# Five hand-written step orders instead of two, and an earlier low part in the tail, in a fused attention and expert kernel

## The chip, the cores and the metric

The kernel runs on one core of a Trainium2 chip. The metric is the device time of one execution in microseconds (us). The engines are TensorE (PE, with its weight loads PEld), VectorE (DVE), ScalarE (ACT), GpSimd (POOL) and SyncE (SP, which issues DMAs). Every engine works through its own instructions in the order in which the program gives them.

## The reference

Three layers: attention that keeps the 32 largest scores of each row, a gated feed-forward layer, and a layer in which each token goes to one of eight experts. Batch 4, 8 heads, 576 positions, head size 64; 2304 tokens of width 512.

```python
scores = scale * q @ k.T                                # 32 x (576 x 576)
kth = np.partition(scores, -32, axis=-1)[..., -32:-31]
scores = np.where(scores >= kth, scores, -1e9)
attn = softmax(scores); x = attn @ v                    # 2304 x 512
h = x @ w_in                                            # 512 -> 2048
y = (h * np.clip(h + 3, 0, 6) / 6) @ w_out              # 2048 -> 512
logits = norm(y) @ norm(expert_emb).T / tau             # 8 experts
e = logits.argmax(1); gate = softmax(logits)[e]
out = gate * (np.maximum(y @ w1[e], 0) @ w2[e])         # 512 -> 1024 -> 512
```

## The kernel before

The attention is cut into 72 units: 128 query rows of two heads each (the last eight units hold the rows left over). A software pipeline runs over them in steps i = 0 to 75. Step i works on six units at once: it computes the scores of unit i, picks the 32 largest values of unit i-1, masks unit i-2, takes the exponentials and sums of unit i-3, turns unit i-4 so that its keys lie on partitions, and in odd steps multiplies units i-5 and i-4 with v. After every eight units (step 11 is the first time) a group of 256 tokens is complete; it gives eight pieces of the feed-forward layer, and from step 12 on (step 13 excepted) each step also does one piece. In steps 0 to 18 the feed-forward weights are prepared too: 32 pieces ("pairs" of row blocks) are rounded to a high part, which stays in SBUF, and a low part, which goes to DRAM and is fetched when needed; a step handles two of them (one in steps 0 to 2).

A step is a list of named operations, and the list is a hand-written string: `FIRST` for steps 0 to 11, `MID` for steps 12 to 20, then `ODD` and `THEN` alternately. The names are issued in the string's order, so that the string sets, for every engine and for SP's DMA queue, what stands ahead of what. The names:

- weights: `load` (DMA), `one` and `two` (DVE, lines 245 and 252, write tile wf), `round` (ACT, 260), `add` (POOL, 265), then one step later `hi` (ACT, 273), `low` (POOL, 277), `store` (DMA). The digit behind is which of the step's two pieces.
- attention: `score0/1` (PE, the two halves of the keys), `take0/1` (ACT copies out of PSUM, 450), `pairs` (DVE, 459 to 463, folds the halves), `pick0..3` (DVE, MAX8 and MATCH_REPLACE, 478 and 481), `bounds` (POOL), `bend0/1` (ACT, 492, tile z), `mask0/1` (POOL, 496), `expo0/1` (ACT, 502), `guard` (POOL, 506), `inverse` (DVE, 509), `scale` (ACT, 516; POOL from unit 16), `turn0..2` (PE, 529), `keep0..2` (ACT, 534, tile pt), `values` (PE, 547), `xh` (ACT, 564), `xl` (DVE, 579).
- feed-forward: `s10`, `s11` (PE, 611), `gate` (ACT), `swish` (DVE, 623), `large` (ACT), `small` (POOL), `s20`, `s21` (PE, 646).
- `lows`, `ship`, `prep`, `need_v`, `load_k`, `load_q` prepare keys, queries and values.

The two halves of a unit's scores share one PSUM tile. `score0` of step i+1 therefore waits until `pairs` and `take1` of step i are through with it. The lists name `pairs` behind `take1`; in step 0 alone two lines of `step` put it ahead:

```python
        if i == 0:
            names.remove("pairs")
            names.insert(names.index("take1"), "pairs")
```

Behind the steps comes the tail: the last group's feed-forward pieces, the routing of its 256 tokens (`choose`, `rank`, `place`), and the first expert. `hidden(0, f, ...)` is one block of 128 hidden features of the first expert (12 matmuls into tile ph, of which there are two), `hidden_out` reads ph (ACT, line 971, and DVE, line 972, the low part hl), and `first` is both. `split_2(0, k)` splits a quarter of the expert's second weights into a high part h (ACT, 869) and a low part l (DVE, 871); the weights a come by DMAs that are issued earlier (line 865).

Of the kernel before, what the change touches and what calls it, by code (L numbers as in the profile page):

```python
# [40 lines left out]

PAUSE = (13,)
RAMP, MOES, WORDS = 3, 12, 21
FIRST = ("hi0 s10 expo0 lows hi1 turn0 one0 s11 s20 low0 round0 two0 ship keep0 turn1 expo1 guard bend0 keep1 add0 turn2 load0 "
         "store0 one1 load_k inverse keep2 prep mask0 pick0 round1 score0 gate take0 scale two1 bend1 load_q swish large values xh "
         "score1 pick1 pick2 aside s21 add1 load1 xl pick3 need_v low1 take1 store1 pairs mask1 bounds small")
MID = ("lows turn0 hi0 turn1 low0 s10 s11 ship keep0 one0 keep1 expo0 two0 pick0 load_k turn2 store0 one1 pick1 expo1 hi1 guard "
       "round0 bend0 two1 score0 pick2 keep2 low1 s20 take0 gate bend1 inverse add0 score1 values take1 round1 scale swish mask0 "
       "large s21 add1 xh pick3 need_v prep xl mask1 load_q bounds small store1 load0 load1 pairs aside")
THEN = ("lows pick0 turn0 expo0 keep0 ship expo1 pick1 bend0 s10 guard turn1 place pick2 inverse score0 mask0 turn2 s11 take0 "  # L50
        "keep1 bend1 pick3 need_v gate load_k score1 swish keep2 scale aside load_q bounds values take1 mask1 xh large xl prep "
        "s20 small s21 pairs")
ODD = ("pick0 turn0 bend0 pick1 turn1 lows s10 s11 keep0 ship score0 expo0 keep1 gate pick2 mask0 turn2 place keep2 bend1 mask1 "
       "take0 swish values expo1 load_k score1 guard need_v pick3 bounds take1 large aside inverse s20 s21 scale small xh pairs "
       "prep xl load_q")
# [47 lines left out]
def layers(tc: tile.TileContext, qt, kt, v, w_in, w_out, embt, tau, w1, w2, out, y_dram, yq_dram, g_dram, tbl, xq_dram, lo_dram, flag, pools, consts):  # L103
# [40 lines left out]
    def bank():  # L144
        turn[1] ^= 1
        return bank_t[turn[1]]
# [603 lines left out]
    def rank():  # L750

        g0, g1 = open_.popleft()
        n = g1 - g0
        pq = (bank() if looping[0] else half_a())[:, :n * E]
        nc.tensor.matmul(pq, tri, picks[:, g0:g1, :].rearrange("p g e -> p (g e)"), start=True, stop=False)
        nc.tensor.matmul(pq, ones, before[:, g0:g1, :].rearrange("p g e -> p (g e)"), start=False, stop=True)
        po = fs.tile([128, NG, E], F32, tag="df", name="pos")[:, :n, :]
        nc.vector.tensor_tensor(po, pq.rearrange("p (g e) -> p g e", e=E), ebase.unsqueeze(1).broadcast_to([128, n, E]), op=ALU.add)
        nc.vector.tensor_tensor(po, po, picks[:, g0:g1, :], op=ALU.mult)
        de = fs.tile([128, NG], F32, tag="nrm", name="de")[:, :n]  # L760
        nc.vector.tensor_reduce(de, po, axis=AX.X, op=ALU.add)
        nc.vector.tensor_copy(rows[:, g0:g1], de)
        spots.extend(range(g0, g1))
        done_groups[0] = g1
# [118 lines left out]
    def step(i, last):  # L883
        a = moe.popleft() if moe and i not in PAUSE else None

        def at_(j, f, *a):
            if 0 <= i - j < NU:
                f(i - j, *a)

        def both(f):  # L890
            if i % 2:
                at_(5, f)
                at_(4, f)

        def aside():
            if side:
                side.popleft()()

        def after(o):
            if last:  # L900
                last[6](last[0], o)

        ops = dict(load_k=lambda: load_k(i + 2), load_q=lambda: load_q(i + 3), need_v=lambda: (at_(2, need_v), at_(3, rest_v)), lows=lows, ship=ship, prep=lambda: need_k(1, i - 1) if i in (1, 2) else prep(i + 2),
                   s10=lambda: part(a, 1, 0), s11=lambda: part(a, 1, 1), gate=lambda: lows() if i in (1, 2) else part(a, 2), swish=lambda: part(a, 3), large=lambda: part(a, 4), small=lambda: part(a, 5),
                   s20=lambda: after(0), s21=lambda: after(1), aside=aside, place=place,
                   guard=lambda: at_(3, guard), inverse=lambda: at_(3, inverse), scale=lambda: at_(3, scale), bounds=lambda: at_(1, bounds),
                   pairs=lambda: at_(0, pairs), values=lambda: both(values), xh=lambda: both(finish), xl=lambda: both(finish_low))
        for name, j, f, n in (("bend", 2, relu, 2), ("mask", 2, mask, 2), ("expo", 3, expo, 2), ("pick", 1, select, 4),
                              ("turn", 4, turned, 3), ("keep", 4, keep, 3), ("score", 0, scores, 2), ("take", 0, take, 2)):
            for k in range(n):  # L910
                ops[name + str(k)] = lambda j=j, f=f, k=k: at_(j, f, k)
        def pair(f, j, c):
            n = pair_of(i - j, c)
            if n >= 0:
                f(n)
        for name, f, j in (("load", w_load, -1), ("one", w_one, 0), ("two", w_two, 0), ("round", w_round, 0), ("add", w_add, 0),
                           ("hi", w_hi, 1), ("low", w_low, 1), ("store", w_store, 1)):
            for c in range(2):
                ops[name + str(c)] = lambda f=f, j=j, c=c: pair(f, j, c)
        names = (FIRST if i < MOES else MID if i < WORDS else ODD if i % 2 else THEN).split()  # L920
        if i == 0:
            names.remove("pairs")
            names.insert(names.index("take1"), "pairs")
        for name in names:
            ops[name]()
        if i in (4, 18, 19, 20, 21):
            embed((4, 18, 19, 20, 21).index(i))
        if i == 0:
            load_k(16)
            load_k(17)  # L930
        if i == 24:
            setup()
        if i == 10:
            fetch(0, 0)
            fetch(1, 0)
        return a

    if True:
# [17 lines left out]
        def hidden(r, f, c0, c1, ks=(0, 1, 2, 3)):  # L956
            xh_, xl_ = tok[r]
            h1, l1 = ws1[r]
            if r not in hs:
                hs[r] = [hp.tile([128, 8, CAPS[0]], F32R, tag=t, name=t) for t in ("hh", "hl")]  # L960
            if 0 in ks:
                xt_[f] = late["ph"].tile([128, 512], F32, tag="ph", name="ph2")[:, :c1 - c0]
            ph = xt_[f]
            for k in ks:
                for n, (l, x) in enumerate(((h1, xh_), (h1, xl_), (l1, xh_))):
                    nc.tensor.matmul(ph, l[:, k, 128 * f:128 * f + 128], x[:, k, c0:c1], start=(k == 0 and n == 0), stop=(k == 3 and n == 2))

        def hidden_out(r, f, c0, c1):
            hh, hl = hs[r]
            ph = xt_.pop(f)  # L970
            nc.scalar.activation(hh[:, f, c0:c1], ph, AF.Relu)
            nc.vector.scalar_tensor_tensor(hl[:, f, c0:c1], ph, 0.0, hh[:, f, c0:c1].bitcast(F32), op0=ALU.max, op1=ALU.subtract)

        def first(r, f, c0, c1):
            hidden(r, f, c0, c1)
            hidden_out(r, f, c0, c1)
# [112 lines left out]
        def split_2(r, k, part=None):  # L1089
            if k == 0 and part != 1:  # L1090
                ws2[r] = (ws2[r], [wb.tile([128, 8, DM], F32R, tag=t, name=t, bufs=2) for t in ("h2", "l2")])
            a2, (h2, l2) = ws2[r]
            split(h2[:, 2 * k:2 * k + 2, :], l2[:, 2 * k:2 * k + 2, :], a2[:, 2 * k:2 * k + 2, :], part)
            if k == 3 and part != 0:
                ws2[r] = (h2, l2)
# [72 lines left out]
        with tc.manual_schedule():  # L1168
# [26 lines left out]
            C = (0, 256)  # L1195
            yts = []
            hidden(0, 0, *C)
            for o, (t, g) in enumerate(finals):
                pp = px.tile([128, 4, 128], F32, tag="px", name="pxt")
                for k in range(4):  # L1200
                    nc.tensor.transpose(pp[:, k, :], t.rearrange("p (x k) -> p k x", k=4)[:, k], ident)
                yts.append(gp.tile([128, 4, 128], F32, tag="ob", name="ytl"))
                nc.scalar.copy(yts[o], pp)
                hidden(0, 1, *C, (2 * o, 2 * o + 1))
# [13 lines left out]
            nc.vector.tensor_reduce(l_all[:, NG - 2:NG, :], p2.rearrange("p (o k e) -> p o e k", o=2, k=4)[:, :, :E, :], axis=AX.X, op=ALU.add)  # L1218
            choose()
            hidden(0, 2, *C, (2, 3))  # L1220
            split_2(0, 0)
            hidden(0, 3, *C, (0, 1))
            rank()
            place()
            late["df"] = df = fs.tile([128, NG, E], F32, tag="df", name="df")
# [1 line left out]
            place()  # L1227
            assert done_groups[0] == NG
            load_ids(0, 2, 4)
            hidden_out(0, 2, *C)  # L1230
            hidden(0, 3, *C, (2, 3))
            hidden_out(0, 3, *C)
            split_2(0, 1)
            for f in (4, 5):
                split_2(0, f - 2)
                first(0, f, *C)
            for n in (2, 3):
                get(0, bl[0][n])
            for r in TURNS[1:]:
# [182 lines left out]
```

## Time and profile before

| | |
|---|---|
| median of 3 runs | 1007.3 us (1007.24 to 1010.03) |
| the profiled execution | 1010.28 us, its span 1008.4 us |
| granted TensorE clock over the span | 0.967 |
| busy share of the span | PE 93%, DVE 77%, ACT 71%, POOL 63% |

The span goes from the first to the last instruction in one profiled execution; it is 1.9 us shorter than that execution's own time. Busy shares are means over stages that differ, so they are read by stage.

### The profile page before, as it was taken

The numbers are of one execution on the slowest core, as the hardware profiler recorded it, in microseconds if no ns is written. First come the engines' busy times: TensorE is split into PE (matmuls) and PEld (weight loads), VectorE is DVE, ScalarE is ACT, GpSimd is POOL, SyncE is SP. The second block draws the span as 40 slices with busy tenths as digits, with TensorE's granted clock in tenths as the row PEclk, the third lists the DMA queues.
The fourth block names the chain that finished last, engine by engine and source line by source line (L and its number), as shares of the span: only waits on it lengthen the run. The fifth ranks groups of instructions, "written<-read, shape, count | busy, mean of one in ns | idle before, by whom it ended". The sixth has DMA issues, their size and how long they took to land. (4 is left out here: it accounts for less than half of the span.)

```text
span 1008.4 us, 20692 instructions
## 1 busy us (share of the span) xinstructions
PE 935.6 (93%) x7130; PEld 821.5 (81%) x7130; DVE 778.4 (77%) x2364; ACT 713.2 (71%) x1443; POOL 636.1 (63%) x786
## 2 busy tenths in 40 slices
PE   3656788999999999999999999999999999999997
PEld 1434577989899998998999988889898998998986
DVE  7999999899989989889999899881234455566661
ACT  5899889888889788798787787684335544555551
POOL 5889999677778788688687775675332553024210
PEclk9975799999999999999999999999999999999998
DMA  7655776654455654456564475386595578665640
GB/s 253 208 176 161 228 240 225 217 185 143 149 180 185 236 184 141 154 165 224 187 186 150 137 259 188 121 245 189 173 286 190 134 245 279 232 234 170 226 158 23
DMA packets 100690, 193.22 MB, mean 192 GB/s; under 512 B 16189, under 2 KB 42448, under 8 KB 100575
## 3 DMA queue, kind: packets, MB, share of 16 engines
q1 hardware_dynamic: 95983, 181.74, 55.7%
q0 software_dynamic: 4448, 10.00, 3.1%
q8 instruction: 58, 0.95, 0.4%
q14 instruction: 57, 0.47, 0.1%
q10 hardware_dynamic: 144, 0.07, 0.0%
HBM read 163.64 MB, written 24.92 MB: 187 GB/s over the span
## 5 line engine op out<-in xcount | busy, mean ns | idle before, releaser
L496 POOL TENSOR_TENSOR s<-s,z 128x576 f32<-128x576 f32 x144 | 191.6, 1332 | 62.0 <-ACT z L492 61.4
L611 PE MATMUL bank_h<-xh,vh 128*128 128x256 f32 x576 | 171.5, 298 | 0.0
L611 PE MATMUL bank_h<-xh,lo 128*128 128x256 f32 x576 | 163.9, 285 | 0.0
L611 PE MATMUL bank_h<-xl,vh 128*128 128x256 f32 x576 | 163.8, 284 | 0.0
L478 DVE MAX8 A<-left 128x8 f32<-128x288 f32 (+1 forms) x288 | 159.6, 595 | 0.0
L529 PE MATMUL bank_t<-both,s 128*128 128x128 f32 x648 | 107.8, 290 | 29.6 <-ACT pt L534 18.1
L529 PEld LDWEIGHTS bank_t<-both,s 128*128 128x128 f32 x648 | 81.2, 148 | 51.8 <-ACT pt L534 23.9
L534 ACT COPY pt<-bank_t 128x384 f32<-128x384 f32 x216 | 101.3, 478 | 26.7 <-PE bank_t L529 26.4
L630 POOL TENSOR_TENSOR gl<-u,gh 128x512 fp32r<-128x512 f32 x72 | 92.9, 1290 | 41.3 <-ACT gh L627 41.2
L646 PE MATMUL y<-wh,gh 128*128 128x512 f32 x288 | 116.7, 405 | 0.0
L450 ACT COPY s<-ps_sc 128x576 f32<-128x576 f32 x143 | 92.1, 644 | 33.2 <-PE ps_sc L443 11.3
L492 ACT ACTIVATE z<-s,nb 128x576 bf16<-128x576 f32 x144 | 112.2, 779 | 4.4 <-POOL nb L486 4.3
L502 ACT ACTIVATE s<-s,nb 128x576 f32<-128x576 f32 x144 | 113.0, 785 | 1.1 <-POOL s L496 1.1
L646 PE MATMUL y<-lo,gh 128*128 128x512 f32 x288 | 113.5, 394 | 0.0
L646 PE MATMUL y<-wh,gl 128*128 128x512 f32 x288 | 113.2, 393 | 0.0
L611 PEld LDWEIGHTS bank_h<-xh,vh 128*128 128x128 f32 x576 | 111.2, 193 | 0.5 <-issue 0.2
L611 PEld LDWEIGHTS bank_h<-xl,vh 128*128 128x128 f32 x576 | 111.2, 193 | 0.3
L611 PEld LDWEIGHTS bank_h<-xh,lo 128*128 128x128 f32 x576 | 110.9, 193 | 0.0
L1040 POOL DMA_INDIRECT out_dram<-ob,idt x20 | 24.4, 1220 | 123.4 <-ACT ob L1033 87.5
L518 POOL TENSOR_SCALAR s<-s,sums 128x576 f32<-128x576 f32 x112 | 82.4, 747 | 20.9 <-DVE sums L509 20.4
L547 PE MATMUL bank_a<-pt,vt 128*64 128x128 f32 (+1 forms) x1600 | 94.0, 276 | 0.7 <-ACT pt L534 0.6
L619 ACT ACTIVATE u<-bank_h,half 128x512 f32<-128x512 f32 x72 | 49.9, 693 | 61.5 <-PE bank_h L611 56.8
(272 smaller groups left out, 2614.4 us busy)
## 6 DMA issues: line engine op xcount, KB each, us to landing
lo<-lo_dram SPq DMA_DIRECT2D x144, 512.0 KB
a<-in_moe_w_dram SPq DMA_DIRECT2D x64, 512.0 KB
vt<-in_v_dram SPq DMA_DIRECT2D x28, 320.0 KB
w<-in_moe_w_in_dram SPq DMA_DIRECT2D x16, 512.0 KB
w<-in_moe_w_out_dram SPq DMA_DIRECT2D x16, 512.0 KB
lo_dram<-wf SPq DMA_DIRECT2D x32, 256.0 KB
qraw<-in_q_dram SPq DMA_DIRECT2D x48, 128.0 KB
krs<-in_k_dram SPq DMA_DIRECT2D x16, 288.0 KB
```

The costliest lines, as they stand in the source:

```text
L450: nc.scalar.copy(sbuf[i % NS][:, :, HS * g:HS * g + HS], ps_[i][:, :, :HS])
L478: nc.vector.max(A[:, n, 8 * r:8 * r + 8], src[:, n, :w])
L492: nc.scalar.activation(zb_[n], tile_of(i, n), AF.Relu, bias=sel[i][1][:, n, 1:2], scale=-BIG)
L496: nc.gpsimd.tensor_tensor(s, s, zb_[n], op=ALU.subtract)
L502: nc.scalar.activation(s, s, AF.Exp, bias=sel[i][1][:, n, 0:1], scale=SCALE, accum_out=sums[i][:, n:n + 1])
L518: nc.gpsimd.tensor_scalar(x, x, rv[:, n:n + 1], 1.0, op0=ALU.mult, op1=ALU.mult)
L529: nc.tensor.transpose(pp[:, 128 * k:128 * k + 128], e[:, 128 * (3 * c + k):128 * (3 * c + k) + 128], ident)
L534: nc.scalar.copy(pts[i][:, 3 * c:3 * c + 3, :].rearrange("p k n -> p (k n)"), tb_.pop((i, c))[:, :384])
L547: nc.tensor.matmul(av[64 * n:64 * n + 64, c0:c1], vt[:, k, 64 * n:64 * n + 64], pt[:, k + 5 * n if k < 4 else 4, c0:c1], start=(o == 0), s ...
L611: nc.tensor.matmul(ph[:, a, :], w, x[:, k, :], start=(k == 0 and n == 0), stop=(k == 3 and n == 2))
L630: nc.gpsimd.tensor_tensor(state[q][1], state.pop((q, "u")).rearrange("p (a n) -> p a n", a=2), state[q][0].bitcast(F32), op=ALU.subtract)
L646: nc.tensor.matmul(state["y"][o], x[:, a, c], w, start=(f == 0 and n == 0), stop=(f == 15 and n == 2))
```

## The change

Five lists take the place of two for the first 21 steps: `ZERO` for step 0, `FEW` for steps 1 and 2, a new `FIRST` for steps 3 to 11, a new `MID` for steps 12 to 15 and `NEXT` for steps 16 to 20. No operation is added or removed. The special case of step 0 goes; `ZERO` names `pairs` behind `take1`. `NEXT` names `pairs` ahead of `take1`. In the tail the first `split_2` moves up behind the first `hidden`, the `hidden_out` of block 2 moves ahead of `rank`, and the third and fourth `split_2` go behind the `first` that they stood ahead of.

```diff
-FIRST = ("hi0 s10 expo0 lows hi1 turn0 one0 s11 s20 low0 round0 two0 ship keep0 turn1 expo1 guard bend0 keep1 add0 turn2 load0 "
...
-MID = ("lows turn0 hi0 turn1 low0 s10 s11 ship keep0 one0 keep1 expo0 two0 pick0 load_k turn2 store0 one1 pick1 expo1 hi1 guard "
...
+ZERO = ("hi0 low0 hi1 s10 one0 store0 s20 expo0 one1 low1 round0 turn0 bend1 score0 load_k expo1 guard s11 two0 pick0 keep0 gate "
...
+        "turn2 take1 keep1 ship s21 mask0 pairs large prep small load_q load1 need_v keep2 add1 store1 mask1 ")
...
-        names = (FIRST if i < MOES else MID if i < WORDS else ODD if i % 2 else THEN).split()
-        if i == 0:
-            names.remove("pairs")
-            names.insert(names.index("take1"), "pairs")
+        names = (ZERO if i == 0 else FEW if i < 3 else FIRST if i < MOES else MID if i < 16 else NEXT if i < WORDS else ODD if i % 2 else THEN).split()
...
             hidden(0, 0, *C)
+            split_2(0, 0)
             for o, (t, g) in enumerate(finals):
...
             hidden(0, 2, *C, (2, 3))
-            split_2(0, 0)
             hidden(0, 3, *C, (0, 1))
+            hidden_out(0, 2, *C)
             rank()
...
             load_ids(0, 2, 4)
-            hidden_out(0, 2, *C)
             hidden(0, 3, *C, (2, 3))
             hidden_out(0, 3, *C)
             split_2(0, 1)
             for f in (4, 5):
+                first(0, f, *C)
                 split_2(0, f - 2)
-                first(0, f, *C)
```

Three places show what this does to the engines' queues. (Lines of the changed kernel are numbered 9 higher in the steps and 6 to 9 higher in the tail.)

ACT in step 9, before, from `keep0` to `take1` (pt is the turned unit, z the mask, w a raw weight, ps_sc the scores):

```order
L534 COPY pt<-bank_t_117 128x384
L502 ACTIVATE s_142,sums<-s_142,nb 128x576
L492 ACTIVATE z_146<-s_143,nb 128x576
L534 COPY pt<-bank_t_118 128x384
L534 COPY pt<-bank_t_117 128x384
L260 ACTIVATE w_798<-w_798 128x512
L450 COPY s_141<-ps_sc 128x2x288
L516 ACTIVATE s_142<-s_142,sums 128x576 x2
L492 ACTIVATE z_147<-s_143,nb 128x576
L564 CAST xh<-bank_a 128x128 x2
L450 COPY s_141<-ps_sc 128x2x288
```

ACT in step 9, with the change, from `expo0` and `expo1` (one row) to `take1`:

```order
L511 ACTIVATE s_142,sums<-s_142,nb 128x576 x2
L543 COPY pt<-bank_t_118 128x384
L269 ACTIVATE w_741<-w_741 128x512
L282 CAST wh<-wf 128x512
L501 ACTIVATE z_146<-s_143,nb 128x576
L501 ACTIVATE z_147<-s_143,nb 128x576
L543 COPY pt<-bank_t_117 128x384
L269 ACTIVATE w_787<-w_787 128x512
L459 COPY s_141<-ps_sc 128x2x288
L525 ACTIVATE s_142<-s_142,sums 128x576 x2
L573 CAST xh<-bank_a 128x128 x2
L459 COPY s_141<-ps_sc 128x2x288
```

The last `keep` (the third pt row before, the second of those shown after) now has both `bend` operations (tiles z) ahead of it where it had one; the order of `xh` and `take1` behind it is the same.

DVE in step 14, before, from its start (wf is the weight word that `one` and `two` write, top and left the folded scores, sums the exponentials' sums):

```order
L245 TENSOR_SCALAR wf<-w_1316 128x512
L252 SCALAR_TENSOR_TENSOR wf<-w_1316,wf 128x512
L478 MAX A<-top 128x8 x2
L481 MATCH_REPLACE top<-A,top 128x144 x2
L245 TENSOR_SCALAR wf<-w_1318 128x512
L478 MAX A<-top 128x8 x2
L481 MATCH_REPLACE left<-A,top 128x144 x2
L252 SCALAR_TENSOR_TENSOR wf<-w_1318,wf 128x512
```

DVE in step 14, with the change, from the end of step 13 on (xl belongs to step 13, where it now comes behind `pairs`):

```order
L588 TENSOR_TENSOR xl<-bank_a,xh 128x128 x2
L254 TENSOR_SCALAR wf<-w_1215 128x512
L254 TENSOR_SCALAR wf<-w_1316 128x512
L261 SCALAR_TENSOR_TENSOR wf<-w_1215,wf 128x512
L261 SCALAR_TENSOR_TENSOR wf<-w_1316,wf 128x512
L487 MAX A<-top 128x8 x2
L490 MATCH_REPLACE top<-A,top 128x144 x2
L518 RECIPROCAL sums<-sums 128x2
```

`one0`, `one1`, `two0` and `two1` now stand in one block at the head of the step, where before picks stood between them.

DVE in the tail, before, from the end of `choose` on (spare holds the picks, pos to rows is `rank`, hl is `hidden_out`, l is `split_2`):

```order
L746 TENSOR_TENSOR spare<-eqs,first 128x16
L871 TENSOR_TENSOR l_10112<-a_9975,h_10111 128x1024
L758 TENSOR_TENSOR pos<-bank_a,ebase 128x16
L759 TENSOR_TENSOR pos<-pos,spare 128x16
L761 TENSOR_REDUCE de<-pos 128x2
L762 CAST rows<-de 128x2
L972 SCALAR_TENSOR_TENSOR hl<-ph_10086,hh 128x256
L972 SCALAR_TENSOR_TENSOR hl<-ph_10115,hh 128x256
L871 TENSOR_TENSOR l_10112<-a_9975,h_10111 128x1024 x2
L972 SCALAR_TENSOR_TENSOR hl<-ph_10149,hh 128x256
```

DVE in the tail, with the change, the same stretch:

```order
L755 TENSOR_TENSOR spare<-eqs,first 128x16
L978 SCALAR_TENSOR_TENSOR hl<-ph_10090,hh 128x256
L767 TENSOR_TENSOR pos<-bank_a,ebase 128x16
L768 TENSOR_TENSOR pos<-pos,spare 128x16
L770 TENSOR_REDUCE de<-pos 128x2
L771 CAST rows<-de 128x2
L978 SCALAR_TENSOR_TENSOR hl<-ph_10115,hh 128x256
L880 TENSOR_TENSOR l_10045<-a_9975,h_10044 128x1024
L978 SCALAR_TENSOR_TENSOR hl<-ph_10147,hh 128x256
L880 TENSOR_TENSOR l_10045<-a_9975,h_10044 128x1024
```

The first l row has left this stretch (it now stands ahead of the first hl), the hl row of block 2 stands ahead of `rank`, and one l row instead of two stands ahead of the hl row of block 4.

## Rows read from the trace of the kernel before

**Rows 1.** Busy time by stretch: length, then busy us per engine, clock, DMA share.
```profile
12.00:108.00 96.00, 56.91 (x323) 36.60 (x323) 94.45 (x311) 83.63 (x167) 83.67 (x88) 0.79 0.63 199
108.00:163.00 55.00, 42.38 (x298) 33.52 (x295) 53.72 (x161) 48.95 (x99) 52.15 (x52) 0.88 0.70 234
163.00:700.00 537.00, 535.89 (x4513) 478.27 (x4512) 475.71 (x1634) 434.36 (x937) 401.50 (x554) 1.00 0.57 183
780.00:1008.40 228.40, 218.69 (x1402) 201.28 (x1400) 119.00 (x177) 107.56 (x174) 69.88 (x61) 0.98 0.57 188
```

**Rows 2.** Timeline, DVE and ACT in step 0: start, duration, [idle before, releaser].
```profile
5.22 0.43 DVE L245 TENSOR_SCALAR wf<-w 128x512 int32<-128x512 int32 x1 [4.29 <-DMA w<-in_moe_w_in_dram]
5.68 0.69 DVE L252 SCALAR_TENSOR_TENSOR wf<-w,wf 128x512 int32<-128x512 int32 x1
...
6.50 0.47 DVE L459 TENSOR_TENSOR ps_sc<-ps_sc,s 128x288 f32<-128x288 f32 x1
...
5.79 0.68 ACT L448 COPY s<-bank_t 128x288 f32<-128x288 f32 x2
...
8.95 0.64 ACT L450 COPY s<-ps_sc 128x576 f32<-128x576 f32 x1 [2.48 <-DVE left L463]
```

**Rows 3.** Timeline, DVE: the start of pairs in steps 4, 6, 10 and 12.
```profile
41.28 0.44 DVE L459 TENSOR_TENSOR ps_sc<-ps_sc,s 128x288 f32<-128x288 f32 x1
...
60.34 0.44 DVE L459 TENSOR_TENSOR ps_sc<-ps_sc,s 128x288 f32<-128x288 f32 x1
...
99.54 0.44 DVE L459 TENSOR_TENSOR ps_sc<-ps_sc,s 128x288 f32<-128x288 f32 x1
...
119.38 0.44 DVE L459 TENSOR_TENSOR ps_sc<-ps_sc,s 128x288 f32<-128x288 f32 x1
```

**Rows 4.** Timeline of step 9: ACT, PE and DVE around values.
```profile
82.35 0.84 ACT L534 COPY pt<-bank_t 128x384 f32<-128x384 f32 x2
...
85.56 0.76 ACT L492 ACTIVATE z<-s,nb 128x576 bf16<-128x576 f32 x1
88.10 0.43 ACT L564 CAST xh<-bank_a 128x128 fp32r<-128x128 f32 x2 [1.78 <-PE bank_a L547]
89.01 0.64 ACT L450 COPY s<-ps_sc 128x576 f32<-128x576 f32 x1 [0.47 <-PE ps_sc L439]
...
83.52 4.53 PE L547 MATMUL bank_a<-pt,vt 128*64 128x128 f32 x40
...
88.56 0.49 DVE L579 TENSOR_TENSOR xl<-bank_a,xh 128x128 fp32r<-128x128 f32 x2 [0.55 <-ACT xh L564]
```

**Rows 5.** Groups of one and two, 12 to 180 us, and one case on the timeline.
```profile
L252 DVE SCALAR_TENSOR_TENSOR wf<-w,wf 128x512 int32<-128x512 int32 x30 | 23.9, 798 | 0.5
L245 DVE TENSOR_SCALAR wf<-w 128x512 int32<-128x512 int32 x30 | 15.8, 527 | 0.0
...
143.53 1.67 DVE L252 SCALAR_TENSOR_TENSOR wf<-w,wf 128x512 int32<-128x512 int32 x1
...
143.17 1.48 POOL L277 TENSOR_TENSOR wf<-wf,vh 128x512 fp32r<-128x512 f32 x1
```

**Rows 6.** Timeline of the tail: PE, DVE, ACT and SP around the first expert.
```profile
755.81 2.49 SPq L865 DMA_DIRECT2D a<-in_moe_w_dram  x4
...
765.41 0.59 ACT L1203 COPY ytl<-pxt 128x512 f32<-128x512 f32 x1 [1.37 <-PE pxt L1201]
...
768.44 1.05 ACT L869 CAST h<-a 128x1024 fp32r<-128x1024 f32 x1
...
770.59 1.23 DVE L871 TENSOR_TENSOR l<-a,h 128x1024 fp32r<-128x1024 f32 x1
...
772.42 0.75 DVE L972 SCALAR_TENSOR_TENSOR hl<-ph,hh 128x256 fp32r<-128x256 f32 x2
...
772.89 0.39 PE L966 MATMUL ph<-xh__9917,h 128*128 128x256 f32 x1 [1.13 <-DVE hl L972]
...
776.43 0.39 PE L966 MATMUL ph<-xh__9917,h 128*128 128x256 f32 x1 [0.42 <-DVE hl L972]
```

More of the change, by code (lines that the diff above doesn't have):

```diff
@@ L43 @@
 RAMP, MOES, WORDS = 3, 12, 21
-FIRST = ("hi0 s10 expo0 lows hi1 turn0 one0 s11 s20 low0 round0 two0 ship keep0 turn1 expo1 guard bend0 keep1 add0 turn2 load0 "
-         "store0 one1 load_k inverse keep2 prep mask0 pick0 round1 score0 gate take0 scale two1 bend1 load_q swish large values xh "
-         "score1 pick1 pick2 aside s21 add1 load1 xl pick3 need_v low1 take1 store1 pairs mask1 bounds small")
-MID = ("lows turn0 hi0 turn1 low0 s10 s11 ship keep0 one0 keep1 expo0 two0 pick0 load_k turn2 store0 one1 pick1 expo1 hi1 guard "
-       "round0 bend0 two1 score0 pick2 keep2 low1 s20 take0 gate bend1 inverse add0 score1 values take1 round1 scale swish mask0 "
-       "large s21 add1 xh pick3 need_v prep xl mask1 load_q bounds small store1 load0 load1 pairs aside")
+ZERO = ("hi0 low0 hi1 s10 one0 store0 s20 expo0 one1 low1 round0 turn0 bend1 score0 load_k expo1 guard s11 two0 pick0 keep0 gate "
+       "lows pick1 inverse swish scale pick2 add0 take0 round1 turn1 values xh pick3 score1 bounds xl bend0 two1 load0 aside "
+       "turn2 take1 keep1 ship s21 mask0 pairs large prep small load_q load1 need_v keep2 add1 store1 mask1 ")
@@ new lines @@
+FEW = ("s10 hi1 s11 lows turn0 expo0 expo1 guard hi0 pick0 round1 pick1 bend1 low0 inverse one0 turn1 low1 load_k turn2 ship "
+       "load0 prep keep0 mask1 keep1 s20 bend0 load_q one1 scale two0 values pick2 score0 two1 gate store0 take0 round0 add1 "
+       "score1 aside swish add0 large mask0 load1 need_v xh store1 xl small pick3 take1 bounds s21 pairs keep2 ")
+FIRST = ("one0 turn0 s10 load0 load_k hi0 low0 s20 lows keep0 turn1 expo0 ship s11 expo1 turn2 score0 guard keep1 two0 round0 prep "
+       "gate one1 hi1 bend0 bend1 pick0 two1 aside keep2 swish add0 round1 large inverse low1 mask0 pick1 add1 store0 load1 "
+       "take0 scale s21 mask1 values pick2 need_v xh score1 pick3 load_q small take1 bounds xl pairs store1 ")
@@ new lines @@
+MID = ("one0 hi0 one1 low0 expo0 round0 load0 turn0 two0 keep0 turn1 bend0 two1 expo1 pick0 guard round1 load_k add0 s10 turn2 "
+       "score0 bend1 hi1 inverse mask0 s20 lows s11 take0 low1 keep1 gate pick1 score1 pick2 add1 keep2 values need_v s21 scale "
+       "ship swish pick3 take1 xh prep store0 mask1 large pairs aside load1 bounds store1 xl load_q small ")
+NEXT = ("hi0 turn0 expo0 load0 keep0 round1 turn1 one0 expo1 pick0 s10 s11 bend0 turn2 keep1 pick1 guard two0 load_k inverse "
+       "keep2 round0 score0 low0 hi1 take0 one1 pick2 values store0 s20 mask0 s21 lows gate add0 ship score1 prep xh swish scale "
+       "low1 xl need_v load_q bend1 two1 aside pick3 large mask1 add1 bounds load1 small pairs take1 store1 ")
```

## The prediction

> **What bounds the kernel now.** I read the busy time by stretch first. From 12 to 108 us (steps 1 to 11) DVE is busy 94.45 of 96 us and PE 56.91; from 108 to 163 us (steps 12 to 16) DVE is busy 53.72 of 55, POOL 52.15, ACT 48.95, PE 42.38; from 163 to 700 us PE is busy 535.89 of 537, and from 780 us to the end 218.69 of 228.40 [rows 1]. So DVE, with POOL and ACT close behind, sets the pace until about 163 us, and PE from there on. Whatever moves the moment at which PE becomes the bound moves the end one for one, because PE has next to no idle time behind it that could swallow it.
>
> The same rows say how little is to be had. An order changes no operation, so it can remove only waiting. DVE's idle time is 1.55 us in steps 1 to 11 and 1.28 us in steps 12 to 16 [rows 1]. A second kind of waiting hides inside DVE's busy time: `one` took 0.43 us and `two` 0.69 us where nothing was in their way [rows 2], but the 30 of each from 12 to 180 us have means of 0.527 and 0.798 us [rows 5]. That is 30 x (0.097 + 0.108) = 6.1 us. One case shows what they wait for: a `two` that began at 143.53 us took 1.67 us and ended at 145.20; the POOL operation beside it ran until 144.65, and 0.55 us are left behind that, nearly a `two` undisturbed [rows 5]. Together 1.55 + 1.28 + 6.1, some 9 us or 0.9%, is the most that the new orders could find on DVE up to 180 us.
>
> The Trainium skill, page "SBUF — State Buffer", section "Who interferes with whom", says why such a wait lasts a whole instruction: a DVE operation with two SBUF inputs, or in a two-port mode, and a GpSimd operation lock a shared pair of ports against each other, and the one that issued first keeps it to its end. The trace agrees, by the case just told; the page's rule speaks against the new `MID`, a rival below.
>
> **The change part by part.** Step 0: `pairs` began at 6.50 us, right behind the two copies of `take0` (5.79 to 6.47), and ACT's `take1` waited 2.48 us for it [rows 2]. Now `take1` comes first. It lasts 0.64 us, so `pairs` starts near 7.1: **+0.6 us**, on an engine that has nothing else ready (`one` and `two` of the first piece are done by 6.37, the next piece's stand behind). Bounds: 0, if ACT's freed 2.48 us let DVE catch up later; +1.3, if `two` or a second copy is in the way too. Steps 1 and 2 (`FEW`): the same DVE work without a new partner to wait for; 0, in the bounds of the next term.
>
> Steps 3 to 11: in the early pair of steps, 4 and 5, `pairs` to `pairs` took 60.34 - 41.28 = 19.06 us for two steps; in the late pair, 10 and 11, 119.38 - 99.54 = 19.84 us [rows 3]. The odd steps show where the 0.8 us come from. In step 9 the last two `keep` end at 83.19, `values` starts at 83.52 and takes 4.53 us, `xh` waits 1.78 us for it, `take1` another 0.47 us for the scores behind it, and DVE's `xl` 0.55 us for `xh` [rows 4]. TensorE's mean granted clock in this stretch is 0.79, between its levels of 1.2 and 2.4 GHz [rows 1], which is why `values` is long. So a chain ACT, PE, ACT runs through an odd step: whatever stands ahead of the last `keep` delays `take1`, and with it the next step of ACT. The new `FIRST` moves the second `bend` (0.76 us, at 85.56 behind the last `keep` until now [rows 4]) ahead of it. The gap of 0.33 us between `keep` and `values` (PE was at the scores) takes up a part: 0.76 - 0.33 = 0.43 us for each of the four odd steps 5, 7, 9, 11: **+1.7 us**. `xl` now stands behind the last pick and no longer stalls, which returns up to 0.55 us an odd step where the chain leaves room. Bounds: -2.2 (all four stalls of `xl` gone, 4 x 0.55, nothing lost) and +3.0 (4 x 0.76); I take the middle of the chain because ACT, not DVE, starts the next step.
>
> Steps 12 to 15: DVE has 1.28 us of idle to gain; what `one` and `two` lose is worth at most the 6.1 us, spread over all steps. The new list puts the four of them at the head of the step, where POOL is still at the last step's `mask1` or at `low0`. Undisturbed they need 0.43 x 2 + 0.69 x 2 = 2.2 us; a POOL operation between two of them costs up to 1.67 - 0.69 = 1.0 us [rows 5]. Against that, `xl` goes behind `pairs`, and `inverse` comes earlier, so that `scale`, which PE's next turn waits for, does too. POOL being busy 95%, I expect a wash: **0**, bounds -4 (the idle and nearly half of the locking gone) and +4 (one more blocked operation in each of four steps).
>
> Steps 16 to 20: PE idles 1.1 us of 537 between 163 and 700 us [rows 1], and these steps are its beginning. `values` right behind `score0` and the early `xl` can take up half of it: **-0.5**. The other side: `NEXT` makes ACT's `take1` wait for `pairs` each step, as in step 0 before, where this wait was 2.48 us [rows 2]; PE's next `score0` is behind it, but so are 24 matmuls of `s10` and `s11` that PE does first. Cover gone, five steps at a fifth of that would be +2.5; bounds -1.0 and +2.5.
>
> Tail: PE waits 1.13 us and 0.42 us for the hl rows that free a ph tile [rows 6]. Before the first of them DVE does an l row (1.23 us at 770.59), then `rank`; the hl row starts at 772.42 [rows 6]. In the change that l row is gone from this stretch and the hl row precedes `rank`, so block 4 finds its ph free; behind it one l row instead of two precedes the next hl. Both waits go: **-1.55 us**. What moved needs a place: ACT's h copy (1.05 us at 768.44) now stands ahead of the `ytl` copies, and ACT idled 1.37 us just there [rows 6]; its weights were asked for at 755.81 [rows 6], some 8 us earlier. `rank` and the two `place` DMAs on POOL behind it come sooner too, by about 0.9 us (the l row of 1.23 leaves, an hl row of half 0.75 comes). SP's `load_ids` waits for them, so nothing is queued later. Bounds: -1.6, and +1.5 if that copy has to wait for its weights, since the routing of the last group is behind it.
>
> Sum: 0.6 + 1.7 + 0 - 0.5 - 1.55 = +0.25 us. The profiled execution took 1010.28 us, 3 us above the median of 1007.3; by this sum it would be 1010.5, and the median 1007.55. I predict **1007.6 us**: no difference that can be told (0.3%, 3 us, is about what this measurement can tell).
>
> **The rivals.** (A) Faster: the orders find a good part of the 9 us. For it: the stalls of `xl`, `one` and `two` are real and all lie in steps whose lists are new. Against it: DVE was busy 98% and POOL 95% in the densest stretch, and the port waits are shared, not removed, by moving them. If half of the 9 us is found and the tail keeps its 1.55: 1007.3 - 4.5 - 1.55 + 0.6 = 1001.9 us.
>
> (B) Slower by the port: at the head of each `MID` step the four operations alternate with POOL's. For it: the blocked `two` of rows 5 stood exactly there, behind `one0`. Against it: the picks that stood between them gave POOL its turn at no cost to the count of blocked operations. Two more blocked operations a step, four steps, 1.0 us each: +8, 1015.6 us; it becomes slower than the bound from one a step on (+4, 1011.6).
>
> (C) Slower by the ACT chain: the odd steps cost the full 0.76 us, with the even ones alike because the new list has `scale` between `take0` and `take1`: 9 x 0.76 = 6.8 instead of 1.7, 1012.7 us. It decides from about 0.6 us a step on. For it: ACT is in the chain of rows 4. Against it: in the early pair DVE still set the pace.
>
> (D) The tail's move does nothing or harm: the h copy waits for its weights; +1.5 instead of -1.55 gives 1010.7.
>
> **How the numbers follow.** No change to tell 0.46 (the forecast 0.41, D 0.05), A 0.28, B 0.13, C 0.13. A lies in faster, B and C in slower: 0.28, 0.46, 0.26. The range reaches to A's time less 1.4 us, and to C's plus 0.8, leaving out the better half of A's finds and the dearer part of B: 1000.5 to 1013.5. The forecast's own range is 1004.3 to 1010.6.
>
> **What would show it.** Step 0: `pairs` near 7.1 us, behind a `take1`. Steps 3 to 11: `pairs` of step 12 near 121.5 us (119.38 + 0.6 + 1.7), `xl` without idle, and idle ahead of `pairs` in odd steps. Steps 12 to 15: `one` and `two` with a mean above 0.53 and 0.80 us if B holds. Tail: no PE idle of 1.13 us. I am wrong if `pairs` of step 12 comes before 119, if DVE's `one` and `two` fall to 0.43 and 0.69, or if PE's idle between 108 and 163 us (12.6) shrinks by more than 3.

## The result, and the profile after

The changed kernel takes 1015.16 us in the median (1013.61 to 1016.84, six runs), the kernel before 1007.4 us beside it (1006.31 to 1010.03, six runs): a ratio of 1.0073, 95% interval 1.0059 to 1.0088. It is slower by some 7.8 us, and the prediction of 1007.6 us, range 1000.5 to 1013.5, missed it. The profiled execution took 1014.37 us, its span 1012.6 us. Its granted TensorE clock was 0.974 over the span (0.967 before).

Where the time went is seen from the stages that answer to [rows 1]. Busy time by stretch after the change: length, then busy us of PE, PEld, DVE, ACT and POOL (in brackets the number of instructions), clock, DMA share, GB/s. The last row is the kernel before.

```profile
12.00:108.00 96.00, 54.48 (x306) 35.06 (x308) 95.32 (x306) 83.79 (x165) 82.20 (x87) 0.81 0.61 195
108.00:163.00 55.00, 45.18 (x318) 34.73 (x316) 54.63 (x165) 50.23 (x104) 48.57 (x51) 0.89 0.68 223
163.00:222.00 59.00, 48.91 (x384) 42.61 (x383) 45.45 (x148) 43.66 (x90) 40.87 (x53) 0.97 0.52 165
163.00:700.00 537.00, 526.50 (x4435) 468.06 (x4434) 475.03 (x1629) 429.31 (x926) 398.16 (x548) 1.00 0.56 178
...
163.00:222.00 59.00, 58.00 (x454) 52.19 (x453) 52.93 (x176) 52.76 (x111) 45.09 (x60) 0.97 0.58 192
```

From 163 to 700 us PE idled 10.5 us where it had idled 1.1 [rows 1], and 10.1 of them lie between 163 and 222 us, where it had idled 1.0: this is the stretch from the `pairs` of step 16 (164.58 us) to that of step 21 (220.32 us), where the waits of `NEXT`, the list of steps 16 to 20, take effect. Ahead of that little was lost: DVE's idle is 0.68 and 0.37 us, down from 1.55 and 1.28 [rows 1], and `pairs` of step 16 starts 1.1 us later than before (163.48). The waits of PE and ACT from 163 to 222 us after the change (us in total, times, longest):

```profile
PE bank_t L538 <- ACT pt L543: 8.2, 4, 3.3
PE bank_a L556 <- ACT pt L543: 1.7, 1, 1.7
...
ACT s L459 <- DVE left L472: 13.6, 5, 4.3
ACT s L459 <- PE ps_sc L452: 0.5, 1, 0.5
```

Before the change PE waited 0.6 and 0.4 us here, and `take1` never waited for `pairs`. Now ACT waits 13.6 us, once in each of the five steps, for L472, the last instruction of `pairs`; L459 is `take1`. PE waits for L543, the `keep` copies of ACT. The timeline of ACT, PE and DVE at the seam of steps 16 and 17 shows how one becomes the other:

```profile
163.24 0.62 ACT L636 CAST gh<-u 128x512 fp32r<-128x512 f32 x1
167.00 0.64 ACT L459 COPY s<-ps_sc 128x576 f32<-128x576 f32 x1 [3.13 <-DVE left L472]
167.53 0.62 ACT L282 CAST vh<-wf 128x512 fp32r<-128x512 f32 x1
168.06 0.78 ACT L511 ACTIVATE s<-s,nb 128x576 f32<-128x576 f32 x1
168.82 0.47 ACT L543 COPY pt<-bank_t 128x384 f32<-128x384 f32 x1
...
169.34 0.55 PE L538 MATMUL bank_t<-both,s 128*128 128x128 f32 x3 [3.30 <-ACT pt L543]
169.65 0.38 PE L452 MATMUL ps_sc<-kst,qh 128*128 128x288 f32 x1
...
164.58 0.44 DVE L468 TENSOR_TENSOR ps_sc<-ps_sc,s 128x288 f32<-128x288 f32 x1
166.46 0.45 DVE L472 TENSOR_TENSOR left<-ps_sc,left 128x288 f32<-128x288 f32 x1
```

ACT is ready for `take1` at 163.86 us. DVE begins `pairs` at 164.58 and ends it at 166.91. Behind `take1` on ACT stand `hi0`, `expo0` and `keep0` of the next step, so `keep0` comes at 168.82, and PE's `turn2` (169.34), which needs the PSUM tile that `keep0` empties, has idled 3.30 us by then. `score0` stands behind `turn2`, and the next `pairs` needs the scores: `pairs`, `take1`, `keep0`, `turn2`, `score0` and the next `pairs` form a ring that every step goes round once.

Three more places that the prediction named. `pairs` of steps 0, 1 and 12 on DVE with a word operation of step 1, and the POOL operation beside that one:

```profile
7.23 0.47 DVE L468 TENSOR_TENSOR ps_sc<-ps_sc,s 128x288 f32<-128x288 f32 x1 [0.67 <-ACT s L459]
11.89 1.95 DVE L261 SCALAR_TENSOR_TENSOR wf<-w,wf 128x512 int32<-128x512 int32 x1
16.67 0.44 DVE L468 TENSOR_TENSOR ps_sc<-ps_sc,s 128x288 f32<-128x288 f32 x1
120.36 0.45 DVE L468 TENSOR_TENSOR ps_sc<-ps_sc,s 128x288 f32<-128x288 f32 x1
...
11.88 1.41 POOL L428 TENSOR_TENSOR kraw<-kraw,kst 128x576 fp32r<-128x576 f32 x1 [1.91 <-DVE wf L254]
```

The groups of `two` and `one` from 12 to 180 us (busy, mean ns of one), which answer to [rows 5]:

```profile
L261 DVE SCALAR_TENSOR_TENSOR wf<-w,wf 128x512 int32<-128x512 int32 x31 | 25.0, 818 | 0.4
L254 DVE TENSOR_SCALAR wf<-w 128x512 int32<-128x512 int32 x30 | 16.9, 574 | 0.0
```

And all of PE's waits from 700 us to the end:

```profile
PE ph L972 <- DVE hl L978: 0.4, 1, 0.4
```

`pairs` of step 12 is 1.0 us later than the 119.38 of [rows 3], the means of `one` and `two` from 12 to 180 us are a little higher (in which steps is seen below), and of the tail's waits of [rows 6] one of 0.4 us is left.

### The profile page after: what moved, and what is told of

The parts are those of the page before. It is cut to its first block, busy times and chain, and to the rows that moved or that the text cites. A ratio compares the mean times of both kernels' runs of the same rounds, so it can differ in the third digit from the quotient of the medians.

```text
span 1012.6 us, 20682 instructions
## 1 busy us (share of the span) xinstructions
PE 935.0 (92%) x7130; PEld 819.1 (81%) x7130; DVE 780.5 (77%) x2364; ACT 713.3 (70%) x1443; POOL 628.3 (62%) x786
## 5 line engine op out<-in xcount | busy, mean ns | idle before, releaser
L505 POOL TENSOR_TENSOR s<-s,z 128x576 f32<-128x576 f32 x144 | 186.3, 1294 | 65.3 <-ACT z L501 64.9
L459 ACT COPY s<-ps_sc 128x576 f32<-128x576 f32 x143 | 92.0, 643 | 40.9 <-DVE left L472 13.6
L543 ACT COPY pt<-bank_t 128x384 f32<-128x384 f32 x216 | 102.6, 478 | 23.2 <-PE bank_t L538 22.9
L556 PEld LDWEIGHTS bank_a<-pt,vt 128*64 128x64 f32 x1600 | 85.6, 145 | 11.5 <-issue 7.2
```

Source lines behind the costliest of these rows:

```text
L459: nc.scalar.copy(sbuf[i % NS][:, :, HS * g:HS * g + HS], ps_[i][:, :, :HS])
L505: nc.gpsimd.tensor_tensor(s, s, zb_[n], op=ALU.subtract)
L543: nc.scalar.copy(pts[i][:, 3 * c:3 * c + 3, :].rearrange("p k n -> p (k n)"), tb_.pop((i, c))[:, :384])
L556: nc.tensor.matmul(av[64 * n:64 * n + 64, c0:c1], vt[:, k, 64 * n:64 * n + 64], pt[:, k + 5 * n if k < 4 else 4, c0:c1], start=(o == 0), s ...
```

## The experiments

**The theories.** N: `NEXT` names `pairs` ahead of `take1`, ACT waits there for DVE, and PE behind it for `keep`; without this there is no loss. Against it E: the loss comes from steps before 16 (the port lock in `MID`, which is B of the prediction and whose time of 1015.6 us was nearly the measured one, or ACT's chain in `FIRST`, C). And M: it is the rest of `NEXT`'s order. In the diffs `OLD_FIRST` and `OLD_MID` are the lists of before. The last column is the start of step 71's `pairs` in the profiled execution, behind which only the tail is left; two profiles of the kernel before have it at 670.63 and 670.74.

| run | what it is | median us | ratio to before, 95% | last `pairs` us |
|---|---|---|---|---|
| after | the change | 1015.16 | 1.0073 (1.0059 to 1.0088) | 681.23 |
| e1_old_16_20 | change, old list in 16 to 20 | 1004.4 | 0.9974 (0.9963 to 0.9985) | 672.75 |
| e2_take_first | change, two names swapped | 1002.26 | 0.9952 (0.9938 to 0.9966) | 670.57 |
| e3_only_16_20 | before, `NEXT` alone | 1016.58 | 1.0098 (1.0083 to 1.0113) | 681.67 |
| e10_take_last | before, `take1` moved | 1015.66 | 1.0085 (1.0065 to 1.0104) | 681.74 |
| e4_only_tail | before, tail alone | 1004.45 | 0.9978 (0.9969 to 0.9988) | 671.29 |
| e5_only_0_2 | before, `ZERO`, `FEW` alone | 1008.93 | 1.002 (1.0011 to 1.003) | 673.66 |
| e11_words_early | e5 with a word piece earlier | 1010.11 | 1.0034 (1.0023 to 1.0046) | 675.54 |
| e6_only_3_11 | before, `FIRST` alone | 1005.61 | 0.9982 (0.997 to 0.9993) | 673.11 |
| e7_only_12_15 | before, `MID` alone | 1004.35 | 0.9972 (0.9961 to 0.9983) | 670.12 |
| e8_best | e2, old list in 0 to 2 | 1001.42 | 0.9943 (0.9929 to 0.9957) | 669.06 |
| e12_old_3_11 | e8, old list in 3 to 11 | 1000.92 | 0.9941 (0.9927 to 0.9955) | 669.37 |
| e9_before_again | before, unchanged | 1007.17 | 1.0003 (0.9994 to 1.0012) | 670.74 |

**e1: the old list back in steps 16 to 20.**

```diff
-MID if i < 16 else NEXT if i < WORDS
+MID if i < 16 else OLD_MID if i < WORDS
```

> The changed kernel with the old MID in steps 16 to 20, everything else as changed. Theory N (NEXT lets ACT's take1 wait for pairs, and PE then waits for the keep copies behind it): the 10 us of PE idle between 163 and 222 us go, and the time is 1015.2 - 10 = about 1005 us, under 1008 in any case. Theory E (the loss comes from the steps before 16, by the port in MID or the ACT chain in FIRST): at least 1012 us.

1004.4 us: the loss is gone, and E with it. In the trace the new lists ahead of step 16, with the old one behind them, still cost 2.0 us at the last `pairs`; `NEXT` adds 8.5 us to that.

**e2: the two names swapped.**

```diff
-       "low1 xl need_v load_q bend1 two1 aside pick3 large mask1 add1 bounds load1 small pairs take1 store1 ")
+       "low1 xl need_v load_q bend1 two1 aside pick3 large mask1 add1 bounds load1 small take1 pairs store1 ")
```

> The changed kernel with two names of NEXT swapped, take1 ahead of pairs, and nothing else. Theory N, that this one wait is the cost: ACT's 13.6 us of waiting for the folded scores go, DVE's pairs waits for take1 in some steps instead (up to 1.3 us each, off PE's path), and the time is 1005 to 1008 us. Theory M (it is the rest of NEXT: bend1, scale and xh late): at least 1012 us, with PE still waiting more than 6 us for pt between 163 and 222 us.

1002.26 us, 12.9 under the changed kernel (10.8 between the two profiled executions), by a swap that leaves every engine's own order as it was and only turns round who waits for whom. M falls. The stretch of steps 16 to 20 and the waits of PE in it:

```profile
163.00:222.00 59.00, 56.74 (x454) 51.20 (x453) 54.12 (x179) 52.22 (x110) 47.20 (x61) 1.00 0.64 206
```

```profile
PE bank_a L556 <- ACT pt L543: 1.1, 1, 1.1
PE ps_sc L452 <- DVE left L472: 0.8, 2, 0.4
PE ps_sc L452 <- PE bank_t L538: 0.2, 1, 0.2
```

PE idles 2.3 us there instead of 10.1, and ACT's `take1` no longer waits for `pairs`. DVE pays for it: its `pairs` now waits for the copy, most of all in step 19 (the idle time ahead of it in brackets), and nothing on PE waits long for that:

```profile
193.52 0.47 DVE L468 TENSOR_TENSOR ps_sc<-ps_sc,s 128x288 f32<-128x288 f32 x1 [1.60 <-ACT s L459]
```

**e3: `NEXT` alone in the kernel before.**

```diff
-MID if i < WORDS
+MID if i < 16 else NEXT if i < WORDS
```

> The kernel before with the new NEXT in steps 16 to 20 and nothing else. Theory N: 1007.4 + 8 to 11 = 1015 to 1018 us, ACT waiting 10 us or more for pairs in these steps. Theory E: under 1011 us.

1016.58 us, with the same wait on ACT:

```profile
ACT s L459 <- DVE left L472: 14.7, 5, 4.3
```

**e10: `take1` behind `pairs`, in the old list.**

```diff
-... score1 values take1 round1 scale ... store1 load0 load1 pairs aside
+... score1 values round1 scale ... store1 load0 load1 pairs take1 aside
```

> The kernel before with one name of the old list moved in steps 16 to 20: take1 right behind pairs at the list's end; nothing else. Theory N, that the wait of take1 for pairs is the cost whatever list it stands in: ACT waits some 10 us for pairs, PE idles 5 us or more behind it, 1007 + 5 to 10 = 1012 to 1017 us. Theory M (the rest of NEXT makes the wait dear): under 1010 us.

1015.66 us. One name moved in a list that is otherwise as before costs nearly what all of `NEXT` does. ACT and PE from 163 to 222 us, and the busy time there:

```profile
ACT s L459 <- DVE left L472: 9.0, 5, 2.7
...
PE ps_sc L452 <- ACT s L459: 3.8, 3, 1.8
PE bank_t L538 <- ACT pt L543: 1.7, 1, 1.7
...
163.00:222.00 59.00, 52.59 (x385) 46.46 (x384) 43.47 (x144) 45.03 (x93) 39.23 (x51) 0.88 0.46 154
```

The move does two things: it puts `take1` behind `pairs`, and on ACT also behind `round1`, `scale`, `large` and `xh`. ACT stood ready for 9.0 us in all until `pairs` was done, so the wait itself is there; but PE waits longest for `take1` directly, and how much the later place on ACT adds was not taken apart. A part of the cost is the clock: PE idles 6.4 us in this stretch where it idled 1.0 before, and its granted clock is 0.88 instead of 0.97. So the clean test of N is e2: taken out of `NEXT`, the wait gives 12.9 us back. That a wait of this kind put into the old list costs about 9 agrees with it.

**e4: the tail alone.** Its diff is the tail's part of the change, and the old lists.

> The kernel before with the new tail and nothing else. My term: 1007.4 - 1.55 = about 1005.9 us, and no PE idle of 1.13 us near 773. The opposite (the copy of the split has to wait for its weights, or the end is set elsewhere): 1007.4 or more, up to 1009.

1004.45 us. PE's waits of 1.13 and 0.42 us of [rows 6] have become one of 0.41:

```profile
775.68 0.38 PE L972 MATMUL ph<-xh__9917,h 128*128 128x256 f32 x1 [0.41 <-DVE hl L978]
```

The one that is left lies behind an l row, as before. From the last `pairs` to the last hl row it takes 313.9 or 314.0 us in every kernel with the new tail and 315.3 or 315.4 us in every one with the old, except the first profile of before. That is 1.5 us; the ratio says 1.2 to 3.1.

**e5 and e11: steps 0 to 2 alone, and with a word piece earlier.**

```diff
-OLD_FIRST if i < MOES
+ZERO if i == 0 else FEW if i < 3 else OLD_FIRST if i < MOES
```

> The kernel before with the new lists ZERO and FEW in steps 0 to 2 and nothing else. My term for steps 0 to 2 was +0.6; the changed kernel's trace shows pairs 2.0 us later from step 1 on (0.7 from step 0, and a two of step 1 that took 1.95 us beside a POOL operation). If DVE sets the pace to 163 us, the 2.0 us stay: 1007.0 + 2.0 = 1009.0 us. If slack behind it swallows them: 1007.0 us.

1008.93 us, a ratio of 1.002. `pairs` of step 0 is at 7.05, of step 1 at 16.43, where the second profile of before has 14.72: 1.7 us, still 1.7 at step 40 and 2.9 at the last `pairs`. In step 1 it is `one` that is held up here, beside a POOL operation that ends at 12.60. DVE, then POOL:

```profile
11.27 1.61 DVE L254 TENSOR_SCALAR wf<-w 128x512 int32<-128x512 int32 x1
...
11.19 1.41 POOL L428 TENSOR_TENSOR kraw<-kraw,kst 128x576 fp32r<-128x576 f32 x1 [1.41 <-ACT kst L366]
```

e11 moves that piece ahead in `FEW`:

```diff
-... expo1 guard hi0 pick0 round1 pick1 bend1 low0 inverse one0 turn1 ... scale two0 values ...
+... expo1 guard hi0 one0 two0 pick0 round1 pick1 bend1 low0 inverse turn1 ... scale values ...
```

> The kernel before with ZERO and FEW in steps 0 to 2 (which took 1008.9 us), and in FEW one0 and two0 moved ahead of pick0. Theory P (1.2 of the 1.7 us lost in step 1 are one word operation that waits for POOL's kraw operation at the shared port): no blocked one or two in step 1, pairs of step 1 at 15.3 us instead of 16.4, and 1008.9 - 1.2 = 1007.7 us. Other theory (the late pairs of step 0 carries all of it): pairs of step 1 still near 16.4, 1008.9 us.

In step 1 it went as P had it (`pairs` at 15.57 us), but in step 2 the piece now fell onto POOL's next operations. DVE in step 2, and POOL beside it:

```profile
17.82 1.00 DVE L254 TENSOR_SCALAR wf<-w 128x512 int32<-128x512 int32 x1
18.86 1.77 DVE L261 SCALAR_TENSOR_TENSOR wf<-w,wf 128x512 int32<-128x512 int32 x1
...
17.26 1.28 POOL L505 TENSOR_TENSOR s<-s,z 128x576 f32<-128x576 f32 x1
18.50 1.58 POOL L428 TENSOR_TENSOR kraw<-kraw,kst 128x576 fp32r<-128x576 f32 x1
```

`pairs` of step 2 is at 25.41 against 24.60 in e5, and the time is 1010.11 us. The wait at the port was moved, and grew.

**e6 and e7: `FIRST` alone, `MID` alone.**

```diff
-OLD_FIRST if i < MOES else OLD_MID if i < WORDS
+OLD_FIRST if i < 3 else FIRST if i < MOES else OLD_MID if i < WORDS
```

> The kernel before with the new FIRST in steps 3 to 11 and nothing else. My term: +1.7, 1008.7 us. Theory C (0.76 us in each of nine steps by ACT's chain): 1012.7 us or more. Theory S (the stalls of xl and the waits of the scores go, as pairs gained 0.7 to 1.2 us from step 3 to step 12 in the changed kernel): 1007.0 - 1.0 = 1006.0 us, pairs of step 12 about 1 us earlier than before.

1005.61 us, so C falls: `pairs` of step 12 is at 118.97, 0.4 us ahead of the second profile of before (119.39). But from step 15 to step 18 the old `MID` behind it loses 2.4 us (PE waits 2.5 us for `scale` and 1.9 us for `take1`), and its trace still has the last `pairs` 2.4 us late. Time and trace disagree in sign, so what `FIRST` is worth alone stays open.

```diff
-OLD_MID if i < WORDS
+MID if i < 16 else OLD_MID if i < WORDS
```

> The kernel before with the new MID in steps 12 to 15 and nothing else. My term: 0, 1007.0 us. Theory B (two more blocked operations a step at the port): 1011 to 1015 us. Theory S (PE's turns and scores wait less): pairs of step 15 some 2 us earlier, and 1007.0 - 2 = 1005 us, if the old list behind it keeps what was won.

1004.35 us, so B falls. Its mechanism is not there either: in steps 12 to 15 (109 to 152 us) `one` and `two` together take less time with the new `MID` than before, 5.5 + 5.1 us instead of 7.0 + 5.1. The groups of the kernel before, then those of the changed one, which e7 repeats within 0.003 us an operation:

```profile
L252 DVE SCALAR_TENSOR_TENSOR wf<-w,wf 128x512 int32<-128x512 int32 x8 | 7.0, 871 | 0.1
L245 DVE TENSOR_SCALAR wf<-w 128x512 int32<-128x512 int32 x8 | 5.1, 639 | 0.0
...
L254 DVE TENSOR_SCALAR wf<-w 128x512 int32<-128x512 int32 x8 | 5.5, 721 | 0.0
L261 DVE SCALAR_TENSOR_TENSOR wf<-w,wf 128x512 int32<-128x512 int32 x8 | 5.1, 680 | 0.0
```

`pairs` of step 15 is 1.8 us earlier than in the second profile of before, in step 21 it is level with it, and the last is 0.6 us earlier. The trace shows less of a gain than the ratio.

**e8 and e12: putting it together.** e8 is e2 with the old list in steps 0 to 2, e12 is e8 with the old list in steps 3 to 11 as well.

```diff
-ZERO if i == 0 else FEW if i < 3 else FIRST if i < MOES
+OLD_FIRST if i < 3 else FIRST if i < MOES
```

> The changed kernel with take1 ahead of pairs in NEXT (which took 1002.3 us), and with the old list in steps 0 to 2. If the 2.0 us that ZERO and FEW lose stay to the end: 1002.3 - 2.0 = 1000.3 us. If slack swallows them: 1002.3 us. Theory N is wrong if it is over 1005.

```diff
-OLD_FIRST if i < 3 else FIRST if i < MOES
+OLD_FIRST if i < MOES
```

> The fastest kernel so far (1001.4 us: old list in steps 0 to 2, new lists from 3 on, take1 ahead of pairs in NEXT, new tail) with the old FIRST in steps 3 to 11. If the new FIRST gives 1.7 us, as it did alone: 1003.1 us. If it gives nothing there, 1001.4. My first term (it costs 1.7): 999.7 us.

1001.42 and 1000.92 us: both beat both kernels, and their intervals overlap, so in this company `FIRST` is worth nothing that can be told. What e12 still has of the change, the new `MID`, `NEXT` with `take1` first and the new tail, carries the gain together.

**e9: the kernel before once more, unchanged.**

> The instructions of the kernel before, unchanged, as a second program: a control. Ratio 1.000 with an interval that holds it. Its profile shows whether PE's wait of 2.49 us at 917.90 us, and the 4.3 us by which the first profile of before is longer from the last pairs on than four kernels with the same tail, belong to the program (then they are here again) or to that one execution (then the span is about 1004 to 1005 us).

1007.17 us, ratio 1.0003. Its profiled execution has a span of 1003.4 us and no wait near 917 us, so the 1010.28 us of the first profile were that execution's own. Its trace is what I compared the others with above.

## Why the prediction was wrong, step by step

The step that failed is the one on steps 16 to 20, "-0.5 ... bounds -1.0 and +2.5". With everything else of the change in place the order of the two names costs 12.9 us (e2). The term as a whole, new list against old in these steps, measured +10.8 (the changed kernel against e1) where -0.5 was forecast; the rest of `NEXT` gives some 2 us back (e2 against e1). The prediction had found the wait ("`NEXT` makes ACT's `take1` wait for `pairs` each step, as in step 0 before, where this wait was 2.48 us") and sized it rightly by the step: 13.6 / 5 = 2.72 us. It then took it for covered: "PE's next `score0` is behind it, but so are 24 matmuls of `s10` and `s11` that PE does first". That followed the tile, to the next writer of the scores, and not ACT's queue. Behind `take1` on ACT stand `expo0` and `keep0`, and PE's `turn2` needs `keep0` and stands ahead of `score0`. The matmuls of `s10` and `s11` do lie in front, but PE had done them by 166.0 us. The upper bound, a fifth of the wait in each step, came from no row; the wait of one step taken whole, 5 x 2.48 = 12.4 us, would have come close to it. None of the rivals had this wait as its mechanism, and none of the signs that the prediction named looks at steps 16 to 20.

The Trainium skill, page "PSUM — Partial Sum Buffer", section "PSUM bank collisions raise a hardware error", says that the compiler's back end makes ACT and DVE instructions that touch one PSUM bank and quadrant depend on each other, reads too, and whatever columns they touch. The trace agrees: `take1` only reads the scores, in columns 0 to 287 of its banks, and the instruction of `pairs` that it waits for, L472, only reads too, from column 288 on. The second of the two waits for the first to its end, 2.3 us if `pairs` is first and 0.64 us if `take1` is.

By the start of `pairs` in the traces (the changed kernel against e9, the second profile of before) the loss divides like this: +2.0 us up to step 2, -0.6 to step 11, -2.6 to step 15, +10.5 to step 21, +1.3 to step 71, and -1.5 in the tail. That is 9.0 us, the difference of the two profiled times (1014.37 and 1005.31). Nearly all of the 1.3 us lies in step 22, beside a granted clock of 0.64 from 220 to 223 us.

The other terms:

- Steps 0 to 2, +0.6: `pairs` at 7.23 us as forecast (7.1), but step 1 added 1.3 us by a `two` that took 1.95 us beside a POOL operation, a wait that I had put at nothing ("the same DVE work without a new partner to wait for"). It measured +1.6 in the median (e5).
- Steps 3 to 11, +1.7: not found. `pairs` of step 12 came at 120.36, not 121.5; `xl` lost its idle time as forecast, but the idle time ahead of `pairs` in odd steps is not there. In steps 3 to 11 `pairs` gained on before instead of losing.
- Steps 12 to 15, 0: better by 3 us in the median (e7), by 2.6 us in the changed kernel's trace. The means of `one` and `two` from 12 to 180 us rose (574 and 818 ns against 527 and 798), as the prediction's sign for B asked, but not in these steps: here the sixteen of them take 10.6 us instead of 12.1. Most of what they lost lies in step 1 and in steps 16 and 17. From 108 to 163 us PE's wait for `scale` fell from 8.8 to 3.6 us and its wait for `keep` rose from 0.5 to 5.2.
- Tail, -1.55: 1.5 us in the traces, but not quite as worked out. The wait of 1.13 us went and the one of 0.42 us stayed: with one l row instead of two ahead of it, the hl row still comes 0.4 us late (e4). PE's idle time behind the last `pairs` fell by 1.1 us only; where the other 0.3 to 0.4 us come from was not found.

That the measured time lies at rival B's 1015.6 us is chance: B's mechanism is refuted by e7 and its rows.

## What to carry to other kernels

When an edit makes an engine wait, follow that engine's own queue behind the waiting instruction to the first thing that the bounding engine needs, and size the wait as uncovered unless a row shows the cover still running at that moment. Where two engines have to take turns on a buffer, let the one with the short operation and the long queue behind it go first: a copy of 0.64 us ahead of a fold of 2.3 us costs the folding engine little, the other way round cost 9 to 13 us here. Moving an operation that is held up by another engine need not remove the wait: in e11 the wait that left step 1 came back larger in step 2. And read a changed mean by stage: `one` and `two` were slower over 21 steps and faster in the four that the theory was about.

## What was not expected of the hardware

Up to the last `pairs` two executions of the same instructions agree to 0.1 us (670.63 and 670.74), and seven programs with the old tail take 315.3 to 315.4 us from there to the last hl row, but the first profile of before took 319.7. So in that execution the extra 4.3 us lie in the tail; where the other runs of the kernel before (1004.86 to 1010.12 us) differ is not shown. PE's wait in that execution on the timeline, with ACT's, and the stretches around it (columns as above). The clock of 0.79 and 0.87 lies between the levels of 1.2 and 2.4 GHz; from 918 to 920 us it is 0.50, the lower level, and it is 1.00 from 905 to 915 and from 925 to 935 us:

```profile
917.90 0.58 PE L966 MATMUL ph<-xh__11338,h 128*128 128x256 f32 x1 [2.49 <-DVE hl L972]
...
917.00 0.38 ACT L971 ACTIVATE hh<-ph 128x256 fp32r<-128x256 f32 x1 [2.50 <-remote]
```

```profile
915.00:920.00 5.00, 2.51 (x14) 2.31 (x13) 2.58 (x4) 2.16 (x4) 2.31 (x2) 0.79 0.75 224
920.00:925.00 5.00, 5.00 (x28) 4.52 (x28) 3.60 (x6) 2.81 (x5) 0.95 (x1) 0.87 0.23 65
...
918.00:920.00 2.00, 2.00 (x10) 2.00 (x11) 2.00 (x3) 1.16 (x2) 1.54 (x1) 0.50 0.60 157
```

The clock fell behind a gap of 2.5 us and so made the gap dearer: matmuls of one kind (128x256) that began 0.12 us apart ahead of it began 0.21 us apart from 918.3 to 921.3 us. PE waited for DVE's hl, and DVE for ACT's hh, which idled 2.50 us for something that the profile only calls remote; what that was is not shown. The medians of the kernel before (1006.34 to 1007.4 us) lie 1.0 to 2.1 us above e9's profiled execution (1005.31 us), which is the size of what e6 and e7 leave open.
